# Two row maxima of a later group moved behind the shift rows, with the score banks in one ring, in a hash-masked attention and expert kernel

## The chip, the core and the metric

The kernel runs on one core of a Trainium2 chip. The core has engines that run side by side and meet only through semaphores: TensorE (PE in the profile, with PEld for loading its stationary operand), VectorE (DVE), ScalarE (ACT), GpSimd (POOL), and SyncE (SP), which here only issues DMA transfers. TensorE writes to PSUM, which has eight banks of 512 fp32 columns on 128 partitions; VectorE and ScalarE read PSUM, GpSimd doesn't. Everything else lies in SBUF. The metric is the device time of one execution in microseconds; the median of several runs is compared.

## What is computed

The attention has 4 batches of 8 heads, 768 positions and head size 64. A query may see a key only where the six sign bits of both (their products with a small matrix proj) agree. The attended values of the eight heads form a row of 512 for each of 3072 tokens; each row goes to the one expert of eight whose gate product is largest, through two matrix products with a ReLU between, and is scaled by the gate's probability.

```python
q_bits = (np.einsum('bhsd,dk->bhsk', q, proj) > 0).astype(np.int64)
k_bits = (np.einsum('bhsd,dk->bhsk', k, proj) > 0).astype(np.int64)
...
mask = q_bucket[:, :, :, None] == k_bucket[:, :, None, :]
scores = scale * np.matmul(q, k.transpose(0, 1, 3, 2))
scores = np.where(mask, scores, -1000000000.0)
scores = scores - np.max(scores, axis=-1, keepdims=True)
attn = np.exp(scores)
attn = attn / (np.sum(attn, axis=-1, keepdims=True) + 1e-09)
return np.matmul(attn, v).astype(np.float32)
...
expert_idx = np.argmax(logits, axis=1)
...
h = np.maximum(xe @ w1[e], 0.0)
ye = h @ w2[e]
out[mask] = gate_w[mask, None] * ye
```

## The kernel before

**Groups.** Attention works on pairs of heads, 16 in all, and each pair in two groups of 384 queries: t = 2 × pair + half, 32 groups. The loop over t is written out by hand, and the instructions of TensorE, VectorE and ScalarE keep the order in which they are written (line 762). GpSimd's and SyncE's instructions are ordered by the framework's scheduler. A group stands in the loop as follows.

- presum with VectorE (L277), then what is put at slot "w", then the product with v of the group before (`av`, L308 and L311) into a bank o, then its column sums (`sums`, L287, turned by L290).
- Then a string of letters (L784) that sets the order of the rest: m is a row maximum of the next group (`maximum`, L228 two products into a pair of banks, L229 the reduction), p is a piece of this group (`piece`, L267 and L268 into one bank, L270 the exponential), e evacuates o, i inverts the sums (`invert`, L296 to L298), x turns the product with v into token rows (L339, L340), s makes the shift rows of the next group, digits call what was put at that slot.
- A group has twelve pieces (two heads of six key blocks) and needs six maxima (two heads of three query blocks). After pieces 3, 5 and 9 GpSimd adds exponentials together (L275, L277), which the column sums need.

**Shift rows.** `shift_rows` takes the six maxima of a group, marks rows without a partner (L241), puts the negated maximum beside the marks (L242), turns both with four transposes (L245, L246) into the bank "misc", copies two parts of it out (L249 rows, L250 marks) and sends the rows by DMA into the last row of the operand qa (L252), where the pieces of that group read them.

**Operands.** Each head has four operands of 768 columns in the fast fp32 form, qa, qb, ka and kb: high parts, low parts and code bits. `code_products` (L160) makes the products with proj of the next pair but one at the end of each odd group, `code_signs` (L164, L165) turns them to signs in cr at the start of the next even group, and `head_operands` sends eight pieces of cr by DMA into ka and qa (L176, L177), copies high parts (L178 to L181) and subtracts low parts (L182, L183).

**Banks.** Two pairs of banks take the maxima (ps_s), two single banks the pieces (ps_t), one the product with v (ps_o), and one everything else (ps_m, "misc"): sums, codes, shift rows, token rows, gate products. A bank is taken again when its last reader is done.

After the loop the last group is finished in three parts (L804 to L824), the experts are sorted, and the expert stage follows.

## Time and profile before

| | us |
|---|---|
| median of 3 runs (lowest, highest) | 930.82 (926.26, 930.95) |
| profiled execution, whole | 925.8 |
| its span, from the first to the last instruction | 924.0 |
| TensorE busy | 822.1 (89%) |
| VectorE busy | 561.4 (61%) |
| GpSimd busy | 483.5 (52%) |
| ScalarE busy | 436.8 (47%) |

Busy times are sums over the span, and a busy TensorE isn't TensorE at its peak: its clock is granted in steps, and the profile gives the granted clock beside the busy time of any stretch. In a timeline each row has its start, its length, the engine, the line of the kernel, the operation, what it writes and reads, how many instructions of that kind follow each other, and in brackets how long the engine stood idle before and what ended that. An instruction that waits for a shared resource after it has started shows that as length, not as idle time. Where a row has a count, its length runs from the first to the last of them.

### The profile page before, as it was taken

Reading aid. Unit: us, or ns where it says so; the run is one execution under the profiler, and the core shown is the slowest. Engines: PE = TensorE matmul, PEld = TensorE weight load, DVE = VectorE, ACT = ScalarE, POOL = GpSimd, SP = SyncE. Lnnn points to the kernel's source line nnn. Section 1 sums busy time; section 2 is a strip of 40 time slices with the busy share of each in tenths; the row PEclk is TensorE's granted clock in tenths of the full one; section 3 lists DMA queues with packets and bytes.
Section 4 is the critical chain, followed back from the end, with each engine's and each line's share of the span. In section 5 each row is a group of like instructions: output and inputs, shape, how many; then the busy total and the mean of one; then the engine's idle time right before and its main releaser. Section 6 shows DMA issues by size and latency. Waiting matters only on the chain.

```text
span 924.0 us, 14353 instructions
## 1 busy us (share of the span) xinstructions
PE 822.1 (89%) x5175; PEld 586.9 (64%) x5175; DVE 561.4 (61%) x951; ACT 436.8 (47%) x816; POOL 483.5 (52%) x444
## 2 busy tenths in 40 slices
PE   4679898888988988889889898988999999999997
PEld 1444464455544545446445464547999999999995
DVE  5455466677654587556657865665756466567561
ACT  3545546545555464654645555343424334434440
POOL 3535546355654465564637566555036647545643
PEclk9877899888987989789888898889999999999999
DMA  7472021021310211302103040111664665655641
GB/s 215 134 234 62 21 71 59 20 75 42 103 59 21 73 58 53 94 22 72 58 19 103 14 142 25 26 67 60 181 166 133 184 167 149 187 167 168 197 137 44
DMA packets 55081, 89.67 MB, mean 97 GB/s; under 512 B 9330, under 2 KB 31438, under 8 KB 55000
## 3 DMA queue, kind: packets, MB, share of 16 engines
q1 hardware_dynamic: 47960, 75.86, 28.0%
q0 software_dynamic: 4992, 12.69, 3.9%
q8 instruction: 43, 0.70, 0.3%
q10 hardware_dynamic: 2048, 0.10, 0.1%
q14 instruction: 38, 0.31, 0.1%
HBM read 65.69 MB, written 20.37 MB: 93 GB/s over the span
## 4 chain that ended last, share of the span: by engine, by line
PE 41%; issue 20%; DVE 18%; POOL 13%; DMA 5%; ACT 2%; SPq 0%; POOLq 0%; DVEq 0%; ACTq 0%
PE o L311 16%; POOL y L968 8%; PE s L228 7%; DVE top L229 6%; PE t L267 4%; PE t L268 4%; DVE mt L241 3%; PE misc L287 3%; DMA y<-yo,tags 2%; PE misc L160 2%; PE misc L245 2%; DVE s L296 2%; DVE xr L340 1%; DMA xs<-xr,slot 1%; POOL yo L966 1%
## 5 line engine op out<-in xcount | busy, mean ns | idle before, releaser
L270 ACT ACTIVATE pt<-t 128x384 f32<-128x384 f32 x384 | 170.4, 488 | 121.7 <-PE t L268 116.5
L229 DVE TENSOR_REDUCE top<-s 128x1 f32<-128x768 f32 x192 | 174.7, 946 | 18.5 <-PE s L228 13.3
L275 POOL TENSOR_TENSOR ps<-pt 128x768 f32<-128x768 f32 x64 | 116.5, 1820 | 125.7 <-ACT pt L270 117.3
L311 PE MATMUL o<-pt,vt 128*64 128x384 f32 (+1 forms) x816 | 181.2, 609 | 0.0
L267 PE MATMUL t<-qa,ka 77*128 77x384 f32 x384 | 149.9, 390 | 6.2 <-ACT pt L270 6.2
L268 PE MATMUL t<-qb,kb 128*128 128x384 f32 x384 | 133.6, 348 | 0.0
L311 PEld LDWEIGHTS o<-pt,vt 128*64 128x64 f32 x816 | 70.1, 177 | 97.9 <-issue 97.7
L968 POOL DMA_INDIRECT y<-yo,tags x89 | 103.2, 1159 | 25.2 <-issue 22.6
L228 PE MATMUL s<-ka,qa 76*128 76x512 f32 (+1 forms) x384 | 105.3, 371 | 7.3 <-DVE top L229 2.4
L267 PEld LDWEIGHTS t<-qa,ka 77*128 77x128 f32 x384 | 74.4, 194 | 43.9 <-ACT pt L270 28.1
L183 POOL TENSOR_TENSOR qb<-raw,qa 64x768 fp32r<-64x768 f32 x30 | 55.4, 1863 | 73.6 <-DVE qa L179 67.4
L290 DVE STREAM_TRANSPOSE st<-misc 128x192 f32<-128x192 f32 x32 | 12.2, 382 | 132.7 <-PE misc L287 132.6
L228 PEld LDWEIGHTS s<-ka,qa 76*128 76x128 f32 x384 | 66.9, 199 | 28.1 <-DVE top L229 12.0
L648 DVE TENSOR_TENSOR wlo<-wraw,whi 128x1024 fp32r<-128x1024 f32 x60 | 73.5, 1226 | 16.7 <-ACT whi L643 15.9
L959 PE MATMUL hps<-hh,wlo 128*128 128x436 f32 (+6 forms) x224 | 76.4, 341 | 0.6 <-issue 0.6
L959 PE MATMUL hps<-hl,whi 128*128 128x436 f32 (+6 forms) x224 | 76.3, 341 | 0.0
L959 PE MATMUL hps<-hh,whi 128*128 128x448 f32 (+10 forms) x224 | 76.3, 341 | 0.0
L926 ACT ACTIVATE hh<-hps 128x352 fp32r<-128x352 f32 (+3 forms) x56 | 27.9, 499 | 101.8 <-PE hps L940 94.2
L268 PEld LDWEIGHTS t<-qb,kb 128*128 128x128 f32 x384 | 75.7, 197 | 0.0
L940 PE MATMUL hps<-xh,whi 128*128 128x352 f32 (+3 forms) x224 | 75.0, 335 | 0.0
L940 PE MATMUL hps<-xh,wlo 128*128 128x428 f32 (+6 forms) x224 | 74.8, 334 | 0.0
L940 PE MATMUL hps<-xl,whi 128*128 128x428 f32 (+6 forms) x224 | 74.8, 334 | 0.0
(231 smaller groups left out, 1374.3 us busy)
## 6 DMA issues: line engine op xcount, KB each, us to landing
wraw<-w SPq DMA_DIRECT2D x64, 512.0 KB
raw<-qk SPq DMA_DIRECT2D x30, 384.0 KB
xs<-zrow SPq DMA_DIRECT2D x8, 910.0 KB
vt<-v SPq DMA_DIRECT2D x16, 384.0 KB
vr<-vt SPq DMA_DIRECT2D x16, 384.0 KB
xr<-xs SPq DMA_DIRECT2D x12, 178.8 KB
xr<-xs SPq DMA_DIRECT2D x8, 227.5 KB
y<-yo,tags POOLq DMA_INDIRECT x89
```

Source lines behind the costliest of these rows:

```text
L183: G.tensor_tensor(out=qb[D:P], in0=raw[0:D], in1=bf(qa[0:D]), op=ALU.subtract)
L228: PE.matmul(out=s[:, c0:c1], lhsT=qa[0:KM, qs], rhs=ka[0:KM, c0:c1], start=True, stop=True)
L229: V.reduce_max(out=tops[t][:, i:i + 1], in_=s[:, 0:S], axis=AX.X)
L267: PE.matmul(out=s[:, 0:384], lhsT=ka[0:KM + 1, ks], rhs=qa[0:KM + 1, qs], start=True, stop=False)
L268: PE.matmul(out=s[:, 0:384], lhsT=kb[:, ks], rhs=qb[:, qs], start=False, stop=True)
L270: A.activation(pt[:, kc], s[:, 0:384], AF.Exp, bias=0.0, scale=0.125)
L275: eng.tensor_tensor(out=ps, in0=pt[:, 0:2], in1=pt[:, 2:4], op=ALU.add)
L311: PE.matmul(out=o[hh * D:hh * D + D, qs], lhsT=vt[:, kc, hh * D:hh * D + D], rhs=pts[t][hh][:, kc, qs], start=False, stop=kc == NB - 1)
L648: loeng.tensor_tensor(out=lo[:, i:i + step], in0=cell["t"], in1=bf(hi[:, i:i + step]), op=ALU.subtract)
L940: PE.matmul(out=hps[:, 0:w], lhsT=wt[:, c, fs], rhs=xt[:, c, 0:w], start=n == 0, stop=n == 3 * NDC - 1)
L959: PE.matmul(out=yps[:, 0:w], lhsT=wt[:, f, ds], rhs=ht[:, 0:w], start=n == 0, stop=n == 3 * NFC - 1)
L968: rows_apart("out", G.indirect_dma_start(out=out_seg, out_offset=bass.IndirectOffsetOnAxis(ap=tags[:, i, 0:1].bitcast(I32), axis=0), in_=y ...
```

## The change

- The string of the loop is rewritten. A group now computes maxima 2 to 5 of the next group among its pieces (m) and maxima 0 and 1 of the group after that behind the shift rows (M). The first two of group 1 stand ahead of the loop. Slots 1 to 5 move accordingly.
- The bank of the product with v joins the ring of the pieces: ps_t has three banks, ps_o is gone.
- The marks (L241) and the first operation of the inversion (L296) take their constant from a column of a table in SBUF, as an operation with two tensors.
- The code products move from the end of an odd group to its second slot, and their signs on VectorE follow at once; the scaling on ScalarE stays at the start of the even group.
- The high part of qa is cast on ScalarE instead of VectorE. The casts and subtractions for kb, and the cast for qb, are split off and move to the start of the odd group.
- The DMA of the shift rows is issued from SyncE instead of ScalarE.

```diff
@@ -72,7 +72,7 @@
     ident = const.tile([P, P], F32, name="ident")
     pj2 = const.tile([P, 2, SQ], F32, name="pj2")
     pj = pj2[:, 0]
-    cols = const.tile([P, 6], F32, name="cols")
+    cols = const.tile([P, 8], F32, name="cols")
     wg_sb = const.tile([P, NPAIR, 32], F32, name="wg_sb")
     eoff = const.tile([P, 3, E], F32, name="eoff")
     ids = const.tile([P, B * NB + 7, NG], I32, name="ids")
@@ -101,8 +101,7 @@
     smp = att.enter_context(tc.tile_pool(name="smp", bufs=6))
     gp = att.enter_context(tc.tile_pool(name="gp", bufs=2))
     ps_s = psa.enter_context(tc.tile_pool(name="ps_s", bufs=2, space=PSUM))
-    ps_t = psa.enter_context(tc.tile_pool(name="ps_t", bufs=2, space=PSUM))
-    ps_o = psa.enter_context(tc.tile_pool(name="ps_o", bufs=1, space=PSUM))
+    ps_t = psa.enter_context(tc.tile_pool(name="ps_t", bufs=3, space=PSUM))
     ps_m = psa.enter_context(tc.tile_pool(name="ps_m", bufs=1, space=PSUM))
 
 
@@ -162,25 +161,32 @@
     def code_signs(pr):
         cr = codes[pr] = codep.tile([P, 384], F32R, name="cr")
         V.tensor_scalar(out=cr, in0=cps_of.pop(pr)[:, 0:384], scalar1=0.0, scalar2=cols[:, 0:1], op0=ALU.is_gt, op1=ALU.subtract)
+
+    def code_scale(pr):
+        cr = codes[pr]
         A.activation(cr, bf(cr), AF.Copy, bias=0.0, scale=cols[:, 1:2])
 
     def new_operands():
         return [opp.tile([P, S], F32R, name=n) for n in ("qa", "qb", "ka", "kb")]
 
-    def head_operands(pr, hh):
+    def head_first(pr, hh):
+
         raw, cr = raws_of[pr][hh], codes[pr]
-        qa, qb, ka, kb = new_operands()
-        operands[2 * pr + hh] = (qa, qb, ka, kb)
+        qa, qb, ka, kb = operands[2 * pr + hh] = new_operands()
         for x in range(2):
             r, cs = SQ * (2 * hh + x), slice(384 * x, 384 * x + 384)
             SY.dma_start(out=bf(ka[D:D + NC1, cs]), in_=bf(cr[r + NC1:r + 2 * NC1]))
             SY.dma_start(out=bf(qa[D:KM, cs]), in_=bf(cr[r:r + NCODE]))
         A.copy(out=ka[0:D], in_=raw[D:P])
-        V.tensor_copy(out=qa[0:D], in_=raw[0:D])
+        A.copy(out=qa[0:D], in_=raw[0:D])
+        G.tensor_tensor(out=qb[D:P], in0=raw[0:D], in1=bf(qa[0:D]), op=ALU.subtract)
+
+    def head_second(pr, hh):
+        raw = raws_of[pr][hh]
+        qa, qb, ka, kb = operands[2 * pr + hh]
         A.copy(out=kb[D:P], in_=raw[D:P])
+        G.tensor_tensor(out=kb[0:D], in0=raw[D:P], in1=bf(kb[D:P]), op=ALU.subtract)
         A.copy(out=qb[0:D], in_=raw[0:D])
-        G.tensor_tensor(out=kb[0:D], in0=raw[D:P], in1=bf(kb[D:P]), op=ALU.subtract)
-        G.tensor_tensor(out=qb[D:P], in0=raw[0:D], in1=bf(qa[0:D]), op=ALU.subtract)
 
     KM = D + NCODE
 
@@ -238,7 +244,8 @@
         mt = mts[t % 2]
         top = tops[t].rearrange("p (h j) -> p j h", h=2)[:, :, h0:h1]
         marks = mt[:, :, 0:6].rearrange("p j (c h) -> p j c h", c=3)[:, :, :, h0:h1]
-        V.tensor_scalar(out=marks, in0=top.unsqueeze(2).broadcast_to([P, 3, 3, h1 - h0]), scalar1=-0.5 * BIG, scalar2=None, op0=ALU.is_le)
+        V.tensor_tensor(out=marks, in0=top.unsqueeze(2).broadcast_to([P, 3, 3, h1 - h0]),
+                        in1=cols[:, 6:7].unsqueeze(2).unsqueeze(3).broadcast_to([P, 3, 3, h1 - h0]), op=ALU.is_le)
         V.scalar_tensor_tensor(out=mt[:, :, SQ + h0:SQ + h1], in0=bf(mt[:, :, h0:h1]), scalar=-DROP, in1=top, op0=ALU.mult, op1=ALU.subtract)
         rp = ps_m.tile([P, 512], F32, name="misc")
         for jj in range(3):
@@ -249,7 +256,7 @@
         A.copy(out=r, in_=rp[SQ:SQ + 2, 0:384])
         A.copy(out=shifts[t], in_=rp[0:6])
         for hh in hhs:
-            A.dma_start(out=bf(operands[2 * pr + hh][0][KM:KM + 1, 384 * g:384 * g + 384]), in_=bf(r[hh:hh + 1, 0:384]))
+            SY.dma_start(out=bf(operands[2 * pr + hh][0][KM:KM + 1, 384 * g:384 * g + 384]), in_=bf(r[hh:hh + 1, 0:384]))
 
     pts = {}
     psums = {}
@@ -293,7 +300,7 @@
     def invert(t, inv):
         s = sums_of.pop(t).rearrange("p (h j) -> p h j", h=2)
         s6 = smp.tile([P, 2, 3], F32, name="s6", bufs=2)
-        V.tensor_scalar(out=s6, in0=s, scalar1=0.0, scalar2=float(S), op0=ALU.is_equal, op1=ALU.mult)
+        V.scalar_tensor_tensor(out=s6, in0=s, scalar=0.0, in1=cols[:, 7:8].unsqueeze(2).broadcast_to([P, 2, 3]), op0=ALU.is_equal, op1=ALU.mult)
         V.scalar_tensor_tensor(out=s6, in0=s6, scalar=1e-9, in1=s, op0=ALU.add, op1=ALU.add)
         V.reciprocal(out=inv, in_=s6)
 
@@ -659,7 +666,7 @@
             t = ps_s.tile([P, 1024], F32, name="s")
             first_h.extend((t[:, 0:512], t[:, 512:1024]))
         elif f > 3:
-            pool, name = ((ps_o, "o"), (ps_t, "t"), (ps_m, "misc"), (ps_t, "t"))[f - 4]
+            pool, name = ((ps_t, "t"), (ps_t, "t"), (ps_m, "misc"), (ps_t, "t"))[f - 4]
             first_h.append(pool.tile([P, 512], F32, name=name))
         return first_h[f]
 
@@ -697,16 +704,17 @@
 
     for e in range(E):
         put(1 + e // 2, 3 + e % 2, partial(prefill, e))
-    put(0, 1, partial(code_products, 1))
+    put(0, 1, partial(code_products, 1), partial(code_signs, 1))
     for pr in range(NPR):
         t, w = 2 * pr, "w" if pr else 1
         if pr + 1 < NPR:
-            put(t, w, partial(code_signs, pr + 1), partial(head_operands, pr + 1, 0), partial(head_operands, pr + 1, 1))
+            put(t, w, partial(code_scale, pr + 1), partial(head_first, pr + 1, 0), partial(head_first, pr + 1, 1))
             put(t, 2, partial(load_v, pr + 1))
-            put(t + 1, "w", partial(sum_v, pr + 1))
+            put(t + 1, "w", partial(head_second, pr + 1, 0), partial(head_second, pr + 1, 1), partial(sum_v, pr + 1))
         if pr + 2 < NPR:
             put(t, 2, partial(load_raw, pr + 2))
-            put(t + 1, 6, partial(code_products, pr + 2))
+            put(t + 1, 2, partial(code_products, pr + 2), partial(code_signs, pr + 2))
+
     def start_route(t):
         b, g = t // (2 * NPAIR), t % 2
         r = route(b, g)
@@ -773,18 +781,22 @@
     shift_rows(0, (1,))
     first_q(0, 1)
     first_q(1, 1)
+    maximum(1, 0)
+    maximum(1, 1)
     for t in range(NT):
         if t:
             presum(t - 1, 1, 1, V)
             run_at(t, "w")
-            o = ps_o.tile([P, 512], F32, name="o")
+            o = ps_t.tile([P, 512], F32, name="t")
             av(t - 1, o)
             sums(t - 1)
         nm = np_ = 0
-        for x in "mmepp0mpp1mppi2mp3pmp4pxpps56":
-            if x == "m" and t + 1 < NT:
-                maximum(t + 1, nm)
+        for x in "epp1mpp2mipp3mpp4mppxp5psMM6":
+            if x in "mM":
                 nm += 1
+                u, i = (t + 1, nm + 1) if nm < 5 else (t + 2, nm - 5)
+                if u < NT:
+                    maximum(u, i)
             elif x == "s" and t + 1 < NT:
                 shift_rows(t + 1)
             elif x == "p":
@@ -803,7 +815,7 @@
     assert not at
     t = NT - 1
     presum(t, 1, 1, V)
-    o = ps_o.tile([P, 512], F32, name="o")
+    o = ps_t.tile([P, 512], F32, name="t")
     inv2, (c0, c1, c2) = last_route(t, o)
     av(t, o, slice(0, P))
     c0.pop(0)()
@@ -1159,7 +1171,9 @@
     a["w2"] = np.ascontiguousarray(moe_w2.reshape(E, F, NG, NDC, SQ).transpose(0, 1, 3, 2, 4).reshape(E, F, DM))
     a["ident"] = np.eye(P, dtype=np.float32)
     a["tri"] = np.triu(np.ones((P, P), np.float32), 1)
-    cols = np.zeros((P, 6), np.float32)
+    cols = np.zeros((P, 8), np.float32)
+    cols[:, 6] = -0.5 * BIG
+    cols[:, 7] = S
     cols[:, 1] = cols[:, 3] = 1.0
     cols[0:D, 4] = cols[D:P, 5] = 1.0
     for r in range(0, P, SQ):
```

## The prediction

> **What bounds the kernel now.** I read the page first, then one windows view by stage.
>
> ```profile
> span 924.0 us, 14353 instructions
> ...
> PEclk9877899888987989789888898889999999999999
> ```
>
> ```profile
> 49.70:620.00 570.30, 498.08 (x3300) 290.61 (x3302) 364.38 (x598) 302.30 (x596) 315.24 (x276) 0.86 0.20 62
> 620.00:924.00 304.00, 294.72 (x1802) 281.16 (x1792) 171.84 (x312) 112.55 (x184) 146.55 (x144) 0.99 0.52 149
> ```
>
> The columns are length, then busy time of PE, PEld, DVE, ACT, POOL, then granted clock, DMA share, GB/s. The expert stage (from 620) has PE at 97% and a clock of 0.99; the diff touches nothing in it. The 32 groups of the attention loop take 570.3 us with PE busy 498.1, so it idles 72.2 us there, and the clock is 0.86. All that the change can win is in those two numbers. The list of waits says what the idle time is:
>
> ```profile
> PE misc L245 <- DVE mt L242: 51.6, 33, 2.3
> PE misc L160 <- ACT marks L250: 16.2, 14, 1.2
> PE t L267 <- ACT pt L270: 6.2, 5, 5.3
> ```
>
> Two waits make most of it: the transposes of the shift rows wait for mt (1.56 us each), and the code products wait for the evacuation of the only "misc" bank (1.16 us each, 14 times: every odd group up to t = 27). To see what makes mt late I read the timeline of an even group, from the end of the column sums to the next product with v:
>
> ```profile
> 265.77 0.98 PE L228 MATMUL s<-ka,qa 76*128 76x512 f32 x4
> 266.43 3.68 DVE L229 TENSOR_REDUCE top<-s 128x1 f32<-128x768 f32 x4
> 266.59 0.35 PE L267 MATMUL t<-qa,ka 77*128 77x384 f32 x1
> ...
> 269.45 1.84 POOL L275 TENSOR_TENSOR ps<-pt 128x768 f32<-128x768 f32 x1 [2.03 <-ACT pt L270]
> ...
> 272.10 0.88 ACT L270 ACTIVATE pt<-t 128x384 f32<-128x384 f32 x2 [0.33 <-PE t L268]
> ...
> 273.18 1.81 POOL L275 TENSOR_TENSOR ps<-pt 128x768 f32<-128x768 f32 x1
> ...
> 273.31 0.34 PE L268 MATMUL t<-qb,kb 128*128 128x384 f32 x1
> ...
> 273.84 1.18 DVE L241 TENSOR_SCALAR mt<-top 128x18 fp32r<-128x18 f32 x1
> 275.05 0.17 DVE L242 SCALAR_TENSOR_TENSOR mt<-mt,top 128x6 fp32r<-128x6 f32 x1
> 275.37 0.49 PE L245 MATMUL misc<-ident,mt 128*34 128x128 f32 x3 [1.71 <-DVE mt L242]
> ...
> 275.89 0.35 PE L308 MATMUL o<-marks 6*64 6x384 bf16 x2
> ```
>
> Take Z = 265.77, where PE has finished the sums. PE runs through the two first maxima (0.82 us), twelve pieces and four maxima, and is done at Z + 7.88. POOL makes three additions back to back from Z + 3.68 to Z + 9.22. The 18-element L241 starts at Z + 8.07 and ends at Z + 9.25, 0.03 after POOL's last addition: it does not compute for 1.18 us, it waits for POOL. So mt is bound by **the first addition on POOL plus three additions**, and PE's transposes follow 5.92 us after that first addition starts. The odd group adds the code products:
>
> ```profile
> 282.68 0.97 PE L228 MATMUL s<-ka,qa 76*128 76x512 f32 x4
> ...
> 292.22 0.49 PE L245 MATMUL misc<-ident,mt 128*34 128x128 f32 x3 [1.66 <-DVE mt L242]
> ...
> 293.34 0.57 ACT L250 CAST marks<-misc 6x512 bf16<-6x512 f32 x1
> ...
> 293.97 1.51 PE L160 MATMUL misc<-raw,pj 128*32 128x384 f32 x8 [1.16 <-ACT marks L250]
> ...
> 295.41 0.53 PE L308 MATMUL o<-marks 6*64 6x384 bf16 x2
> ```
> ```profile
> 302.93 0.96 PE L228 MATMUL s<-ka,qa 76*128 76x512 f32 x4
> ```
>
> From Z to the product with v are 10.12 us in the even group and 12.73 in the odd one; the product and sums then take 6.79 us (275.89 to 282.68) and 7.52 (295.41 to 302.93). The pair takes 37.16 us. Why 7.52 and not 6.79 is in the windows view, cut at the steps of the granted clock:
>
> ```profile
> 273.13:276.55 3.42, 1.71 (x12) 0.81 (x13) 3.01 (x5) 1.41 (x4) 1.86 (x2) 1.00 0.01 2
> 276.55:279.96 3.41, 3.41 (x14) 1.43 (x12) 0.00 (x0) 1.45 (x3) 1.11 (x7) 0.50 0.14 14
> ...
> 290.20:293.62 3.42, 0.95 (x6) 0.35 (x5) 2.71 (x5) 1.62 (x4) 1.64 (x1) 1.00 0.00 0
> 293.62:297.03 3.41, 3.06 (x14) 0.85 (x16) 1.48 (x3) 1.10 (x3) 0.18 (x1) 0.50 0.01 1
> 297.03:300.44 3.41, 3.41 (x14) 1.23 (x12) 0.06 (x1) 3.34 (x5) 3.41 (x2) 0.50 0.07 17
> ```
>
> A window of 3.41 us in which PE was busy 1.71 is followed by one at half clock. The odd group's longer idle time is followed by two. Half a window of PE work, 1.7 us, is lost in each fully used one.
>
> **The change part by part.** The sum is made against the profiled execution: 925.8 us, of which 924.0 are the span. The median of the runs is 930.82, 0.5% above.
>
> *Maxima ahead.* Two maxima leave the front of the group (0.82 us on PE from 265.77 to 266.59) and stand behind the shift rows. Nothing is computed less. In front, the pieces and POOL's first addition come 0.82 earlier: Z + 2.86, so the transposes stand at Z + 2.86 + 5.92 = 8.78, and PE, done at 7.06, still waits 1.7. Behind, the transposes (275.37 to 275.89, 0.52) and the moved maxima (0.82) bring the product with v to Z + 10.12. That is the time of before: **gain in an even group 0**. VectorE does these two reductions in the product's time, where it did nothing (0.00 busy in 276.55:279.96). In front it has 1.84 us less to do (two of the four in 3.68). It gains less than that, because the inversion still meets POOL's first addition; I put its arrival at L241 at about Z + 7.4 in place of 8.07. POOL's last addition ends at 2.86 + 5.54 = Z + 8.40, so it waits there. What is late next is therefore POOL, not VectorE.
>
> *Two-tensor forms.* L241 and the first operation of the inversion (L296) read a column instead of a constant. The rows to compare are operations with two tensors in SBUF that met POOL:
>
> ```profile
> L241 DVE TENSOR_SCALAR mt<-top x33: 155/1190/1481, 12.5 to 608.6; 128x18 fp32r<-128x18 f32 x31, 128x9 fp32r<-128x9 f32 x2
> ```
> ```profile
> L277 DVE TENSOR_TENSOR ps<-ps,pt x32: 949/957/2936, 48.2 to 631.6; 128x768 f32<-128x768 f32 x32
> ```
> ```profile
> L382 DVE TENSOR_TENSOR oh<-oh,eoff x7: 183/184/1740, 184.2 to 629.7; 128x24 f32<-128x24 f32 x7
> ```
> ```profile
> 335.05 3.69 POOL L183 TENSOR_TENSOR qb<-raw,qa 64x768 fp32r<-64x768 f32 x2 [5.02 <-DVE qa L179]
> ...
> 337.04 1.74 DVE L382 TENSOR_TENSOR oh<-oh,eoff 128x24 f32<-128x24 f32 x1
> ```
>
> L382 takes 0.18 us alone and 1.74 beside POOL, ending at 338.78 with POOL's instruction (338.74). The two-tensor form waits just as L241 does, so I take **0**; the other end is that L241 falls to its 0.16 us, a rival below. The Trainium skill agrees with these rows in "SBUF — State Buffer", section "Who interferes with whom": a VectorE instruction with two SBUF inputs contends with a GpSimd one that reads SBUF. Its page "VectorE: DVE Perf Modes", section "Mode 2×_2P", says only that tensor_tensor cannot use both read ports for one tensor; whoever reads no further expects the wait to go, and by that the sum would be the rival's.
>
> *Code products.* In 14 odd groups they move from the end (wait 1.16, then 1.51 at half clock) to the second slot, between pieces, at full clock: about 0.75, an estimate, half of 1.51. There they delay pieces 4 to 9. POOL's last addition needs the exponentials that ended at 272.98, Z + 7.21; in the new order they end at 7.21 − 0.82 + 0.75 = 7.14, where POOL is free at 2.86 + 3.73 = 6.59: 0.55 lost. The product with v stands at Z + 10.12 + 0.55 = 10.67 instead of 12.73: 2.06 gained. PE is done at 7.06 + 0.75 and waits until 8.78 + 0.55; this wait of 1.5 us resembles the even group's, so I take one half-clock window, not two: 7.52 becomes 6.79, 0.73 gained. **14 × 2.79 = 39 us.** The signs follow on VectorE:
>
> ```profile
> 295.55 0.62 DVE L164 TENSOR_SCALAR cr<-misc,cols 128x384 fp32r<-128x384 f32 x1 [2.61 <-DMA qa<-rows]
> ```
>
> These 0.62 us stand in front of L241, which then starts at about Z + 8.0 and has until 8.95 under POOL. Without that cover they would cost up to 14 × 0.62 = 8.7.
>
> *Casts.*
>
> ```profile
> L178 ACT CAST ka<-raw 64x768 fp32r<-64x768 f32 x30 | 24.9, 830 | 0.7
> ```
> ```profile
> L179 DVE CAST qa<-raw 64x768 fp32r<-64x768 f32 x30 | 15.9, 569 | 0.0
> ```
>
> qa goes from VectorE (0.57) to ScalarE (0.83 like ka's), and kb and qb move an odd group later. ScalarE has 4 × 0.83 in either group in place of 6 and 0, POOL two subtractions in either in place of four and none; both lie under the product's 6.8 us. Only in group 0 do they stand in front of the exponentials (the wait of 5.3 in the list above): 2 × 0.83 = **1.7 us gained** once. Without the cover, 0.83 × 30 = 25 us would be lost.
>
> *Third bank in the ring.* PE waits for a bank visibly only 6.2 us in all, 5.3 of them that first one, and POOL's chain hides the rest: 0, at most about 0.2 per group.
>
> *Rows on SP.*
>
> ```profile
> 335.04 0.81 SPq L176 DMA_DIRECT2D ka<-cr  x1
> ...
> 340.83 0.73 SPq L177 DMA_DIRECT2D qa<-cr  x1
> ```
> ```profile
> L252 ACTq DMA_DIRECT2D qa<-rows x64: 504/524/1531, 14.5 to 612.1; - x64
> ```
>
> ScalarE's queue loses 2 × 0.52 us per group, hidden. On SP the two transfers stand beside eight issues that take 6.5 us. Ahead of them they cost nothing; behind them, see the last rival. I take 0, since the rows are ready before the codes.
>
> Sum: 39 + 1.7 = 41; 925.8 − 41 = 885.
>
> **Rivals.**
>
> *The clock stays up (831 to 866).* The remaining wait is 1.5 to 1.7 us. Where it straddles two windows, neither shows 1.71 busy and no half clock follows. All 32 escaping would save 32 × 1.7 = 54 (831), half of them 27 (858). For it: the idle time is shorter than before in odd groups. Against it: the even group's 1.71 triggered it. By the Trainium skill, "TensorE: Matmul & The Clock Gate", section "Why this matters for your kernels", only gaps above about 3 us bring half rate, which would give 831; the trace shows half rate after a wait of 1.71.
>
> *The two-tensor form does not wait (about 783).* L241 would end about Z + 7, 1.5 us earlier, the wait fall to some 0.2, and the half clock go: 32 × (1.5 + 1.7) = 102, 885 − 102 = 783. Against it: the rows of L277 and L382.
>
> *Two half windows remain (about 902).* If the wait's tail reaches into the slow window, an odd group still loses 0.73 to 1.7: 14 × 1.2 = 17.
>
> *No difference (about 926).* The change does not do what it says: the third maximum, the signs and the inversion keep VectorE, not POOL, ahead of mt, by the 2.8 us that an odd group gained; nothing is left but group 0's 1.7, which is within what can be told.
>
> *Slower: rows queue behind the codes on SP (about 943).* If SP takes the rows after the eight codes, they are issued some 9.8 us after the transposes (1.7 to the end of marks, 0.6 for the scale, 6.5 for the codes, 1.0 of their own) and land about 2.2 later (an estimate: marks begin at 293.34 as the rows' cast ends, and L164 above is released by their landing at 295.55); the first piece wants them at 0.52 + 0.82 + 6.79 = 8.1. That is 3.9 us in 15 even groups: +58. It decides from an issue later than 5.9 us after the transposes.
>
> **How the numbers follow.** Forecast 0.56 (866 to 900), clock up 0.16, two-tensor 0.06, two half windows 0.09, no difference 0.06, slower 0.07. Leaving out two-tensor, no difference and slower (0.19) the range is 835 to 920. Faster by over 0.5% 0.87, within 0.06, slower 0.07; 0.5% is what runs of before differ by (926.26 to 930.95) and about what can be told. I give 885.
>
> **What would show it.** Right: L241 still near 1.2 us and ending with POOL's addition; no wait of L160 for L250; one half-clock window per group; pairs of about 34.3 us; the stage from 620 on as long as now. Wrong: a first piece that waits for qa's rows (SP), L241 at 0.2, or a clock above 0.9 in the attention stage.

## The result, and the profile after

The change made the kernel faster. In the first series its median is 892.85 us (four runs, 889.81 to 901.97) against 928.54 before, a ratio of 0.9633 with a 95% interval of 0.9553 to 0.9714. In a second series, beside partial versions, it is 886.27 us (six runs, 883.01 to 886.62) against 922.17: 0.9592 (0.9565 to 0.9618). The forecast was 885.

The profile is that of a run of the second series (886.62 us). Its page, the heading and the parts on busy time and granted clock:

```profile
span 884.8 us, 14398 instructions
...
PE 781.6 (88%) x5175; PEld 593.2 (67%) x5175; DVE 551.8 (62%) x921; ACT 457.1 (52%) x846; POOL 493.1 (56%) x444
...
PEclk9899989988999898988998899889999999999999
```

The windows view from the start of the first to the start of the last product with v (the third part of the last group's), and behind it, of the kernel before and then of the changed one. Its columns are length, then busy time of PE, PEld, DVE, ACT, POOL, then granted clock, DMA share, GB/s.

```profile
49.23:637.52 588.29, 513.06 (x3447) 301.07 (x3447) 371.58 (x629) 309.18 (x611) 325.06 (x284) 0.86 0.20 62
637.52:924.00 286.48, 280.21 (x1647) 270.84 (x1646) 164.64 (x281) 106.03 (x168) 136.74 (x136) 1.00 0.54 153
```

```profile
45.55:599.10 553.55, 473.16 (x3443) 306.33 (x3443) 366.77 (x602) 330.86 (x642) 336.30 (x287) 0.89 0.22 69
599.10:884.00 284.90, 279.22 (x1647) 271.00 (x1646) 164.32 (x281) 106.00 (x168) 139.09 (x136) 0.99 0.54 155
```

The loop is 34.7 us shorter, what stands before it 3.7, and what stands behind it, up to the end of the span, 0.8. In the loop PE's busy time fell by 39.9 us for the same products, while its idle time rose from 75.2 to 80.4 (length less busy). The gain in the loop is a higher clock, not less waiting. The waits say the same:

```profile
PE misc L252 <- DVE mt L249: 76.6, 32, 5.3
```

The code products (now L159) no longer stand in PE's list of waits, and no wait for the shift rows' transfer does; the wait for mt rose from 51.6 to 76.6 us. The timeline of an even group (Z = 101.97) and the odd one behind it (Z = 118.64) shows what mt waits for:

```profile
106.56 1.85 POOL L284 TENSOR_TENSOR ps<-ps,pt 128x768 f32<-128x768 f32 x1
...
108.37 1.80 POOL L282 TENSOR_TENSOR ps<-pt 128x768 f32<-128x768 f32 x1
...
109.02 1.19 DVE L247 TENSOR_TENSOR mt<-top,cols 128x18 fp32r<-128x18 f32 x1
...
110.56 0.49 PE L252 MATMUL misc<-ident,mt 128*34 128x128 f32 x3 [2.38 <-DVE mt L249]
...
111.78 0.35 PE L315 MATMUL t<-marks 6*64 6x384 bf16 x2
...
120.54 0.85 PE L159 MATMUL misc<-raw,pj 128*32 128x384 f32 x8
```

L247, the former L241, starts under POOL's last addition and ends with it (110.21 and 110.17), in its form with two tensors too. The code products take 0.85 us in place of 1.51, at full clock.

For the experiments I read the end of the column sums of every group off each timeline, and sum up by pairs of groups. **Plain pairs** are eight without routing. **Route pairs** are six in which the gate and the sorting of a finished batch stand (t = 7 to 10, 15 to 18, 23 to 26). "Start" is the first product with v. "Half" counts windows of 3.41 us at half clock in the loop, from the clock in the trace. The ratios leave out runs at a lower granted clock that took over 1.5% more than the fastest of their kernel (three of the six with the casts back, one in each of three other rows), and the last four columns of the row marked * come from such a run, of 854 us where the others took 841 to 852, so they aren't compared with other rows.

| kernel | ratio to before (95%) | plain pairs, mean us | route pairs, mean us | start | half |
|---|---|---|---|---|---|
| before | 1 | 36.9 | 38.5 | 49.2 | 49 |
| changed | 0.9592 (0.9565, 0.9618) | 32.9 | 38.1 | 45.6 | 37 |
| codes alone | 0.9840 (0.9815, 0.9865) | 34.8 | 38.5 | 49.2 | 39 |
| changed, codes back | 0.9797 (0.9752, 0.9843) | 35.0 | 38.1 | 46.0 | 45 |
| changed, casts back | 0.9873 (0.9830, 0.9915) | 35.9 | 37.7 | 50.1 | 45 |
| changed, banks back | 0.9750 (0.9713, 0.9788) | 34.4 | 37.8 | 47.2 | 40 |
| changed, constants and rows back | 0.9565 (0.9521, 0.9608) | 33.1 | 36.7 | 46.3 | 34 |
| changed, maxima back | 0.9546 (0.9518, 0.9573) | 34.0 | 35.7 | 45.2 | 32 |
| the same, casts back too | 0.9661 (0.9613, 0.9708) | 34.4 | 35.0 | 48.8 | 35 |
| before, third addition on VectorE | 0.9271 (0.9225, 0.9316) | 31.6 | 36.6 | 48.0 | 21 |
| changed, third addition on VectorE * | 0.9125 (0.9099, 0.9150) | 29.5 | 37.3 | 45.6 | 33 |
| maxima back, third addition on VectorE | 0.8759 (0.8732, 0.8786) | 28.4 | 32.2 | 45.4 | 8 |
| the same, sums of v first | 0.8831 (0.8795, 0.8868) | 28.7 | 32.5 | 45.0 | 12 |

Differences between kernels are given by the ratio, where one point is 9.2 us (a hundredth of the median of before in these series, 922.17 to 923.09). The half windows and pairs are those of one execution each. Of the half windows, 23 stand in plain and 18 in route pairs before, 12 and 18 in the changed kernel.

### The profile page after: what moved, and what is told of

The parts are those of the page before. It is cut to its first block, busy times and chain, and to the rows that moved or that the text cites. A ratio compares the mean times of both kernels' runs of the same rounds, so it can differ in the third digit from the quotient of the medians.

```text
span 900.2 us, 14398 instructions
## 1 busy us (share of the span) xinstructions
PE 799.1 (89%) x5175; PEld 601.0 (67%) x5175; DVE 553.0 (61%) x921; ACT 457.9 (51%) x846; POOL 493.1 (55%) x444
## 4 chain that ended last, share of the span: by engine, by line
PE 41%; DVE 22%; issue 19%; POOL 11%; DMA 4%; ACT 1%; SPq 1%; another core or an unknown queue 0%; POOLq 0%; ACTq 0%; DVEq 0%
PE t L318 18%; POOL y L980 9%; DVE top L235 7%; PE s L234 6%; DVE mt L247 4%; PE t L274 4%; PE t L275 3%; PE misc L294 2%; PE misc L252 2%; DVE s L303 2%; DVE xr L347 2%; DMA y<-yo,tags 2%; PE misc L159 1%; POOL yo L978 1%; PE t L315 1%
## 5 line engine op out<-in xcount | busy, mean ns | idle before, releaser
L235 DVE TENSOR_REDUCE top<-s 128x1 f32<-128x768 f32 x192 | 177.3, 949 | 74.0 <-PE s L234 72.5
L318 PE MATMUL t<-pt,vt 128*64 128x384 f32 (+1 forms) x816 | 182.7, 614 | 0.0
L274 PE MATMUL t<-qa,ka 77*128 77x384 f32 x384 | 140.8, 367 | 2.3 <-ACT pt L277 2.3
L318 PEld LDWEIGHTS t<-pt,vt 128*64 128x64 f32 x816 | 70.8, 178 | 98.3 <-issue 98.0
L234 PE MATMUL s<-ka,qa 76*128 76x512 f32 (+1 forms) x384 | 112.4, 393 | 4.8 <-ACT qa L217 2.0
L188 POOL TENSOR_TENSOR kb<-raw,kb 64x768 fp32r<-64x768 f32 x30 | 64.8, 2180 | 50.4 <-ACT kb L187 43.0
L234 PEld LDWEIGHTS s<-ka,qa 76*128 76x128 f32 x384 | 72.4, 215 | 28.4 <-issue 11.1
L252 PE MATMUL misc<-ident,mt 128*34 128x128 f32 x99 | 19.3, 312 | 74.4 <-DVE mt L249 74.4
```

What stands on the lines that cost most here:

```text
L188: G.tensor_tensor(out=kb[0:D], in0=raw[D:P], in1=bf(kb[D:P]), op=ALU.subtract)
L234: PE.matmul(out=s[:, c0:c1], lhsT=qa[0:KM, qs], rhs=ka[0:KM, c0:c1], start=True, stop=True)
L235: V.reduce_max(out=tops[t][:, i:i + 1], in_=s[:, 0:S], axis=AX.X)
L274: PE.matmul(out=s[:, 0:384], lhsT=ka[0:KM + 1, ks], rhs=qa[0:KM + 1, qs], start=True, stop=False)
L318: PE.matmul(out=o[hh * D:hh * D + D, qs], lhsT=vt[:, kc, hh * D:hh * D + D], rhs=pts[t][hh][:, kc, qs], start=False, stop=kc == NB - 1)
```

## The experiments

Theory: POOL's additions bound mt, and the move of the code products is nearly all of the gain. Rivals: another part brings it, or VectorE bounds mt.

**The codes back in their old place**, from the changed kernel:

```diff
-put(t, w, partial(code_scale, pr + 1), ...
+put(t, w, *([partial(code_signs, pr + 1)] if pr else []), partial(code_scale, pr + 1), ...
-put(t + 1, 2, partial(code_products, pr + 2), partial(code_signs, pr + 2))
+put(t + 1, 6, partial(code_products, pr + 2))
```

> The changed kernel, but the code products stand at the end of the odd groups and the signs at the start of the even ones again, as before the change; all else of the change stays. Theory (the move of the code products is nearly the whole gain): 14 odd groups lose 2.06 to 2.8 us each, so 29 to 39 us of the 36 us gained go: about 920 to 930 us, ratio to the kernel before 0.99 to 1.00; pairs of groups of about 36.5 to 37.2 us, and the wait of the code products for the bank of the shift rows is there again. Rival A (the third bank in the ring, the casts or the moved maxima bring a good part): at most 900 to 910 us, ratio 0.970 to 0.985.

Measured: 903.37 us, 0.9797. That is 2.05 points, 19 us, above the changed kernel: rival A. Plain pairs give back 2.1 us each, route pairs nothing.

**The codes alone**, from the kernel before:

```diff
-    A.activation(cr, bf(cr), AF.Copy, bias=0.0, scale=cols[:, 1:2])
+
+def code_scale(pr):
+    cr = codes[pr]
+    A.activation(cr, bf(cr), AF.Copy, bias=0.0, scale=cols[:, 1:2])
-put(0, 1, partial(code_products, 1))
+put(0, 1, partial(code_products, 1), partial(code_signs, 1))
-put(t, w, partial(code_signs, pr + 1), partial(head_operands, ...
+put(t, w, partial(code_scale, pr + 1), partial(head_operands, ...
-put(t + 1, 6, partial(code_products, pr + 2))
+put(t + 1, 2, partial(code_products, pr + 2), partial(code_signs, pr + 2))
```

> The kernel before with one part of the change alone: code products and signs at the second slot of the odd group. Maxima, casts, banks, rows and constant forms are those of before. Theory (the move of the code products is nearly the whole gain): 14 x (2.06 to 2.79) = 29 to 39 us less than before, ratio 0.958 to 0.97. Rival A (it needs the other parts: casts off VectorE and maxima off the front make the room): the signs and casts now delay mt, ratio 0.975 to 1.0.

Measured: 908.21 us, 0.984: 15 us. The ratio is in rival A's range. The windows of the first six plain groups and of the four route groups behind them, of this kernel, and then of the kernel before:

```profile
55.84:161.54 105.70, 94.62 (x632) 56.13 (x631) 64.87 (x95) 59.74 (x117) 58.25 (x51) 0.89 0.25 77
161.54:239.02 77.48, 66.14 (x456) 38.62 (x455) 56.62 (x100) 41.40 (x82) 44.82 (x40) 0.89 0.20 66
```

```profile
57.03:167.78 110.75, 95.99 (x632) 56.08 (x631) 64.98 (x95) 60.04 (x117) 58.01 (x51) 0.88 0.23 70
167.78:245.98 78.20, 67.19 (x455) 40.10 (x455) 55.26 (x100) 41.73 (x82) 45.08 (x39) 0.87 0.20 66
```

Three plain pairs gain 5.05 us, two route pairs 0.7. The timeline of the first of these route groups (Z = 161.54) shows a part of the reason:

```profile
168.27 0.85 PE L364 MATMUL misc<-ot,wg_sb 128*32 128x384 f32 x8 [0.88 <-DVE cr L164]
```

The gate product takes the only "misc" bank next after the code products and waits until VectorE has read the signs out of it. The exponentials come later by that too, and POOL's third addition starts at Z + 10.13, in place of 8.28 in the same group before; in plain odd groups it is 8.03 in place of 7.29. PE waits so in three of the twelve route groups. So the move works as predicted where nothing else stands, and the route pairs take the gain back. The part put at 39 us is worth 15 to 19, and some 20 must come from parts put at nothing.

**The casts back**: four casts and four subtractions of a pair in the even group, the cast of qa on VectorE.

```diff
-A.copy(out=qa[0:D], in_=raw[0:D])
+V.tensor_copy(out=qa[0:D], in_=raw[0:D])
-put(t, w, ..., partial(head_first, pr + 1, 0), partial(head_first, pr + 1, 1))
+put(t, w, ..., partial(head_first, pr + 1, 0), partial(head_second, pr + 1, 0), partial(head_first, pr + 1, 1), partial(head_second, pr + 1, 1))
-put(t + 1, "w", partial(head_second, pr + 1, 0), partial(head_second, pr + 1, 1), partial(sum_v, pr + 1))
+put(t + 1, "w", partial(sum_v, pr + 1))
```

> The changed kernel, but the four casts and the four subtractions of a pair's heads all stand in the even group again, with the cast of qa on VectorE. Theory (they lie beside the product with v; only group 0 pays): 0 to 3 us slower than the changed kernel, ratio to it 1.000 to 1.003. Rival (four subtractions in a row on POOL delay POOL's first addition, and the second addition on VectorE waits for them, as in the route groups): 15 to 25 us slower, since code products, maxima and what the first runs show leave some 25 us of the gain to the casts, the bank, the rows and the constants.

Measured: 909.95 to 914.81 us in the three runs that aren't left out, 0.9873: 2.8 points, 26 us. The timeline of this kernel around Z = 72.98 shows the mechanism where it is worst:

```profile
67.81 0.35 PE L315 MATMUL t<-marks 6*64 6x384 bf16 x2
...
70.17 1.01 DVE L181 CAST qa<-raw 64x768 fp32r<-64x768 f32 x2
...
70.68 2.19 POOL L188 TENSOR_TENSOR kb<-raw,kb 64x768 fp32r<-64x768 f32 x1 [4.49 <-DMA ka<-cr]
...
72.94 3.63 POOL L182 TENSOR_TENSOR qb<-raw,qa 64x768 fp32r<-64x768 f32 x2
...
76.65 1.87 POOL L188 TENSOR_TENSOR kb<-raw,kb 64x768 fp32r<-64x768 f32 x1
...
78.59 1.82 POOL L282 TENSOR_TENSOR ps<-pt 128x768 f32<-128x768 f32 x1
...
80.92 1.40 DVE L247 TENSOR_TENSOR mt<-top,cols 128x18 fp32r<-128x18 f32 x1
82.25 1.80 POOL L282 TENSOR_TENSOR ps<-pt 128x768 f32<-128x768 f32 x1
82.36 1.71 DVE L249 SCALAR_TENSOR_TENSOR mt<-mt,top 128x6 fp32r<-128x6 f32 x1
...
84.21 0.80 PE L252 MATMUL misc<-ident,mt 128*34 128x128 f32 x3 [4.58 <-DVE mt L249]
```

VectorE casts qa only behind the moved maxima and its own addition. POOL subtracts for kb first here and starts 2.9 us behind the product with v; the four subtractions reach to Z + 5.5. POOL's first addition starts at Z + 5.6 in place of Z + 2.7 (104.65 − 101.97 in the changed kernel's trace), and both operations that make mt wait for an addition each. The transposes start at Z + 11.2.

Of the eight even groups of plain pairs, two are like this; there the product and sums took only 5.2 us, at full clock. In two they took 6.8 us, and the subtractions reach to Z + 3.8. In four they took 7.4 to 8.1 us, partly at half clock, and the first addition starts at Z + 2.7 as in the changed kernel. So the faster the product with v runs, the less it covers. The loop also starts 4.5 us later.

**The banks back**: two in the ring, one for the product with v.

```diff
-ps_t = ...(name="ps_t", bufs=3, space=PSUM)
+ps_t = ...(name="ps_t", bufs=2, space=PSUM)
+ps_o = ...(name="ps_o", bufs=1, space=PSUM)
...
-o = ps_t.tile([P, 512], F32, name="t")
+o = ps_o.tile([P, 512], F32, name="o")
```

> The changed kernel with two banks in the ring of the pieces and one of its own for the product with v again. Theory (a third bank is hidden by POOL's chain of additions): the changed kernel's time within 4 us. Rival (PE runs ahead of ScalarE with the third bank and is done with the pieces earlier, and so starts the maxima and the shift rows earlier): 10 to 25 us slower; pieces end about 0.5 to 1 us later after the sums.

Measured: 898.87 us, 0.975: 1.6 points, 14.6 us. The rival. In plain groups the pieces end at Z + 7.86 and 7.08 (odd and even) in place of 7.17 and 6.20, the transposes start at Z + 9.46 and 8.78 in place of 8.96 and 8.57. The loop also starts 1.7 us later.

**Constants and rows back**, two parts that the prediction put at nothing, undone together:

```diff
-V.tensor_tensor(out=marks, in0=top..., in1=cols[:, 6:7]..., op=ALU.is_le)
+V.tensor_scalar(out=marks, in0=top..., scalar1=-0.5 * BIG, scalar2=None, op0=ALU.is_le)
-V.scalar_tensor_tensor(out=s6, in0=s, scalar=0.0, in1=cols[:, 7:8]..., op0=ALU.is_equal, op1=ALU.mult)
+V.tensor_scalar(out=s6, in0=s, scalar1=0.0, scalar2=float(S), op0=ALU.is_equal, op1=ALU.mult)
-SY.dma_start(out=bf(operands[2 * pr + hh][0][KM:KM + 1, ...
+A.dma_start(out=bf(operands[2 * pr + hh][0][KM:KM + 1, ...
```

> The changed kernel with two parts undone that the prediction put at nothing: the comparison L247 and the first operation of the inversion take a constant again in place of a second tensor, and the rows' transfers stand on ScalarE's queue again. Theory: the changed kernel's time within 4 us, ratio to before 0.955 to 0.964, L247 still near 1.2 us. Rival (the forms with two tensors do not wait for POOL, those with a constant do): 10 us or more slower, ratio above 0.970, L247 longer by 0.3 us or more.

Measured: 883.10 us, 0.9565. Its interval overlaps that of the changed kernel: no difference that can be told. The lines view by source line (shortest, median, longest ns) of this kernel, then of the changed one:

```profile
L247 DVE TENSOR_SCALAR mt<-top x33: 158/1500/2131, 12.4 to 567.8; 128x18 fp32r<-128x18 f32 x31, 128x9 fp32r<-128x9 f32 x2
```

```profile
L247 DVE TENSOR_TENSOR mt<-top,cols x33: 160/1200/2134, 12.4 to 573.2; 128x18 fp32r<-128x18 f32 x31, 128x9 fp32r<-128x9 f32 x2
```

Both forms take 0.16 us when POOL is still and over 1 us beside it. The median of 1.5 for the constant is what the rival expected of L247, but the time isn't: the length is whatever is left of POOL's addition.

**The maxima back in front**:

```diff
-for x in "epp1mpp2mipp3mpp4mppxp5psMM6":
+for x in "MMepp1mpp2mipp3mpp4mppxp5ps6":
-u, i = (t + 1, nm + 1) if nm < 5 else (t + 2, nm - 5)
+u, i = t + 1, nm - 1
-maximum(1, 0)
-maximum(1, 1)
```

> The changed kernel with the two first maxima of the next group at the front of the group again, not ahead of the product with v. Theory (the maxima only change places on PE; POOL's chain of three additions bounds mt either way): same time as the changed kernel within 5 us, ratio to before 0.958 to 0.969, POOL's first addition about 0.8 us later after the sums, the transposes about 0.7 later, and the product with v where it was. Rival (the moved maxima are the gain, since VectorE came too late for mt): ratio above 0.975, and L247 falls to less than 0.5 us because VectorE comes after POOL's last addition.

Measured: 880.35 us, 0.9546, faster than the changed kernel by 0.46 points with intervals that just touch. The net is 4 us against the moved maxima, and it hides two larger parts: moved, they win 1.1 us in each plain pair and lose 2.4 in each route pair. The lines view from 49.7 to 590 us, of the kernel with the maxima back and then of the changed one:

```profile
L188 POOL TENSOR_TENSOR kb<-raw,kb 64x768 fp32r<-64x768 f32 x29 | 52.2, 1815 | 51.1 <-ACT kb L187 26.1 <-DMA xs<-xr,slot 13.8 <-issue 11.2
L284 DVE TENSOR_TENSOR ps<-ps,pt 128x768 f32<-128x768 f32 x31 | 29.6, 956 | 6.0 <-POOL ps L282 6.0
```

```profile
L188 POOL TENSOR_TENSOR kb<-raw,kb 64x768 fp32r<-64x768 f32 x29 | 62.4, 2172 | 46.2 <-ACT kb L187 38.9 <-issue 7.3
L284 DVE TENSOR_TENSOR ps<-ps,pt 128x768 f32<-128x768 f32 x30 | 34.9, 1163 | 0.0
```

Behind the two moved reductions (1.82 us), VectorE's addition L284 comes when POOL subtracts, and both become longer.

**Maxima and casts back**, the last but with the edit of the casts besides:

> The changed kernel with the two first maxima in front (880 us, ratio 0.955) and, besides, the casts and the four subtractions all in the even group, qa's cast on VectorE. Theory (four subtractions of 1.85 us in a row reach past the sums, POOL's first addition comes about 2 us late, in every even group): 20 to 33 us slower than 880, ratio 0.975 to 0.99. Rival (they hurt only together with the moved maxima, since VectorE's additions then fall beside them): ratio 0.955 to 0.965.

Measured: 892.84 us, 0.9661: 1.15 points, 11 us, between the theory and its rival. Its timeline where a plain group's product with v begins:

```profile
101.62 0.45 PE L315 MATMUL t<-marks 6*64 6x384 bf16 x2
101.73 1.02 DVE L181 CAST qa<-raw 64x768 fp32r<-64x768 f32 x2
...
102.51 3.67 POOL L182 TENSOR_TENSOR qb<-raw,qa 64x768 fp32r<-64x768 f32 x2 [1.80 <-DVE qa L181]
```

With the maxima in front VectorE casts qa at once, and POOL starts 0.9 us behind the product with v. In plain groups it is done by Z + 1.4 to 3.1, ahead of its first addition (Z + 3.6 to 3.8). So the casts are worth about 11 us by themselves, and 26 beside moved maxima. Of the 11, 3.6 lie before the first product with v (the profiled run is the fastest, 886.79); where the rest lies the trace doesn't show. Nor was it tried whether qa's cast or the place of the subtractions counts for more.

**POOL's third addition on VectorE**, from the kernel before and no part of the change. It stands beside the product with v, where VectorE has little else to do:

```diff
-presum(t - 1, 1, 1, V)
+presum(t - 1, 1, 0, V)
+presum(t - 1, 1, 1, V)
...
-if np_ in (3, 5, 9):
+if np_ in (3, 5):
```

> The kernel before with one edit that is no part of the change: POOL's third addition of the sums stands on VectorE at the start of the next iteration. Theory (POOL's last addition bounds mt in the kernel before too, by about 1.2 us a group): the transposes come about 1.2 us earlier in 32 groups (38 us), and part of the 49 half-clock windows of 1.7 us goes (0 to 40 us): ratio to before 0.915 to 0.96. Rival (VectorE, with its four reductions behind the sums, bounds mt in the kernel before, and POOL's chain comes to bind only through the change): ratio 0.985 to 1.0.

Measured: 858.61 us, 0.9271: 7.3 points, 67 us, more than the whole change. POOL's additions bound mt before the change too. The lines view of L241, and the timeline of an even group (Z = 239.73), of this kernel:

```profile
L241 DVE TENSOR_SCALAR mt<-top x33: 158/165/1631, 12.5 to 549.7; 128x18 fp32r<-128x18 f32 x31, 128x9 fp32r<-128x9 f32 x2
```

```profile
245.26 1.86 POOL L277 TENSOR_TENSOR ps<-ps,pt 128x768 f32<-128x768 f32 x1
...
247.72 0.17 DVE L241 TENSOR_SCALAR mt<-top 128x18 fp32r<-128x18 f32 x1
...
248.24 0.49 PE L245 MATMUL misc<-ident,mt 128*34 128x128 f32 x3 [0.75 <-DVE mt L242]
```

POOL is done at Z + 7.39 and L241 takes its 0.17 us; PE waits 0.75 in place of 1.71. The half-clock windows fall from 49 to 21.

**The same edit in the changed kernel**:

> The changed kernel with POOL's third addition of the sums given to VectorE, at the start of the next iteration ahead of VectorE's own one, where VectorE has only the two moved maxima. Theory (POOL's last addition holds mt): L247 runs in about 0.2 us when POOL is idle, mt comes 1.2 to 1.5 us earlier in each of 32 groups, PE's wait before the transposes falls to below 0.8 us, and most of the half-clock windows of the attention stage go: 50 to 90 us less than the changed kernel, about 800 to 845 us, ratio to before 0.86 to 0.91. Rival (VectorE itself bounds mt by then: its third maximum, the inversion and the signs): mt comes at most 0.5 us earlier, ratio 0.94 to 0.965. Second rival (the extra addition on VectorE delays the sums): PE waits for VectorE ahead of the column sums, ratio above 0.965.

Measured: 842.90 us, 0.9125, just outside the range of the ratio. L247 falls to 0.17 us in plain groups; in the profiled run, of 854 us, plain pairs take 29.5 us and route pairs 37.3. The timeline beside the product with v ahead of Z = 112.89 shows the new collision:

```profile
108.84 0.95 DVE L282 TENSOR_TENSOR ps<-pt 128x768 f32<-128x768 f32 x1
108.86 5.12 POOL L188 TENSOR_TENSOR kb<-raw,kb 64x768 fp32r<-64x768 f32 x2 [3.87 <-ACT kb L187]
109.89 2.41 DVE L284 TENSOR_TENSOR ps<-ps,pt 128x768 f32<-128x768 f32 x1
```

Behind the moved reductions, both of VectorE's additions stand beside POOL's subtractions.

**The same edit with the maxima back in front**:

> The third addition of the sums on VectorE, as in the run of 842.9 us, and the two first maxima at the front of the group again. Theory (the moved maxima delay VectorE's additions, and the product with v by 0.7 us behind the shift rows): faster than with the maxima moved by 5 to 15 us: 828 to 838 us, ratio to before 0.895 to 0.907. Rival (with POOL's third addition gone, VectorE bounds mt, and there the moved maxima are what helps: two reductions of 0.95 us less between the sums and mt): 10 to 40 us slower, 853 to 880 us, and L247 runs in 0.2 us behind a late third maximum.

Measured: 807.96 us, 0.8759, 114 us less than before and the fastest of all. Neither the theory's range nor the rival's holds it. The clock on its page:

```profile
PEclk9999999999999999999999988999999999999999
```

Eight half-clock windows are left. Against the kernel with the maxima back alone, transposes 1.0 to 1.45 us earlier in some 30 groups (8.44 and 8.51 in place of 9.90 and 9.53) and 24 windows of 1.7 us fewer make 37 + 41 = 78 us; measured are 7.9 points, 73. Next to this, the moved maxima of the change cost 34 us.

**The sums of v first**, one further edit: `sum_v` ahead of `head_second` at slot "w" of the odd group.

> The kernel of 808 us (third addition on VectorE, maxima in front) with the sums of v ahead of the second casts and subtractions in the odd groups. In that kernel the second product of the shift rows waits in three route groups for 2.2 us for POOL's last small operation on v, which stands behind a subtraction and a gather. Theory: that wait goes, 3 x 2.4 = 7 us less and perhaps the half-clock window of these groups: 798 to 803 us, ratio 0.865 to 0.871. Rival (the subtractions, 1 us later on POOL, push its first addition back): same time or slower, ratio 0.875 to 0.885.

Measured: 816.64 us, 0.8831, slower by 0.7 points: the rival. The waits of the kernel without the edit, and then with it:

```profile
PE misc L253 <- POOL v L151: 6.7, 3, 2.2
```

```profile
POOL vh L149 <- ACT vr L146: 45.0, 12, 3.9
PE misc L253 <- POOL v L151: 2.8, 1, 2.8
```

The wait of three route groups becomes one. But POOL, which waited for ScalarE's casts ahead of its subtractions (46.8 us, 12 times, without the edit), now waits for ScalarE's sums of v there, and in most plain odd groups the subtractions start at about Z − 1.6 in place of Z − 2.9. In a route group (timeline of the kernel with the edit, Z = 288.13) the last one stands where the first addition belongs, and mt is made behind that addition, 12 us past Z:

```profile
296.26 1.81 POOL L188 TENSOR_TENSOR kb<-raw,kb 64x768 fp32r<-64x768 f32 x1 [2.19 <-ACT pt L277]
...
298.29 1.80 POOL L282 TENSOR_TENSOR ps<-pt 128x768 f32<-128x768 f32 x1
298.48 1.65 DVE L247 TENSOR_TENSOR mt<-top,cols 128x18 fp32r<-128x18 f32 x1
```

## Why the prediction was right, and where it was wrong

The forecast of 885 us holds: 886 and 893. The sum behind it was 41 us; 34 to 38 were measured (3.67 and 4.08 points). But its terms don't hold, and their errors cancel, so that the total came out is luck. Taken out of the changed kernel one at a time, codes, casts, bank and maxima are worth 19, 26, 15 and −4 us. That is 56 in all, so they don't simply add up either.

**What bounds the kernel** was right. mt comes with POOL's last addition, and taking that addition away is worth 67 us in the kernel before. The stage behind the loop stayed as it was, within 0.8 us.

**Code products, 39 us: mis-sized.** Measured 15 and 19. In plain pairs the step was right: an odd group from Z to the product with v takes 8.96 + 1.23 = 10.19 us (forecast 10.67), the product and sums 6.86 (6.79), and a pair with the codes alone 34.4, as 37.16 − 2.79 says. What failed is the factor: "14 × 2.79" took one plain pair for all, and six of the pairs stand beside routing, where 0.0 was gained (38.5 and 38.5). Eight times 2.1 is 17.

**Casts, 1.7 us: mis-sized, the cover was wrong.** Measured 11 without and 26 with the moved maxima. What stands before the first product with v alone gives 3.6. The prediction said that POOL's subtractions lie under the product's 6.8 us whether two or four stand there. In the kernel before, the four end 1.2 to 2.8 us past Z in plain even groups; they cost nothing only because the first addition starts as late as Z + 3.6. The moved maxima take that room from both sides: the addition starts at Z + 2.7, and the subtractions begin 1.4 to 2 us later behind the product with v than with the maxima in front. In the worst two groups the subtractions reach to Z + 5.5. The two edits belong together.

**Third bank, 0: wrong, 14.6 us.** "POOL's chain hides the rest" fails: with two banks the pieces end up to 0.9 us later. In plain odd groups POOL's third addition, which needs the tenth piece, starts at Z + 7.26 in place of 6.77; in even groups the first already starts 0.2 later, and the chain behind it. The prediction's own sentence that in odd groups the third addition starts 0.55 late for want of exponentials had shown that pieces bound there.

**Maxima, 0: right as a net (4 us lost), by two errors.** Plain pairs gain 1.1 us each: the product with v comes 0.25 us earlier behind Z in either group, not 0, and the rest is three fewer half-clock windows in the eight pairs. Route pairs lose 2.4 each, 1.7 of them by six more half-clock windows (18 in place of 12): the prediction put VectorE's reductions "in the product's time, where it did nothing", read from one plain group. That this is why the route pairs lose is read from the lines above, not tried alone.

**Two-tensor forms, 0, and rows on SP, 0: right,** as far as undoing both at once can tell. No piece waits for the rows, so the slower rival fell. The rival at 783 us, a form that doesn't wait for POOL, fell: L247 still ends with the addition.

**The half clock** was right in size: one window less in each of 14 odd groups would be 35 in place of 49; 37 were counted. But of the 12 windows that went, 11 lay in plain pairs and none in route pairs. The rival of a clock that stays up fell: the loop's is 0.89.

**What it left out:** the new string puts slot 5 ahead of the shift rows, and with it the expert weights' first cast in the last groups. The timeline of the changed kernel, Z = 542.41:

```profile
549.40 1.71 DVE L652 CAST whi<-wraw 128x1024 fp32r<-128x1024 f32 x1
...
551.18 2.34 POOL L655 TENSOR_TENSOR wlo<-wraw,whi 128x1024 fp32r<-128x1024 f32 x1 [0.63 <-DVE whi L652]
551.42 2.13 DVE L247 TENSOR_TENSOR mt<-top,cols 128x18 fp32r<-128x18 f32 x1
...
553.90 0.80 PE L252 MATMUL misc<-ident,mt 128*34 128x128 f32 x3 [5.29 <-DVE mt L249]
```

In the kernel before, the cast (L645) stands behind mt. This last pair takes 40.9 us in place of 37.2. That the order is the cause is read from the rows; it wasn't tried alone. Nor was it tried alone what takes the gain of the route pairs back.

## What to carry to other kernels

Price a moved step in every kind of iteration that the trace has, since a gain from the quiet ones is given back where other work already fills the gap. When two engines hold each other up at a shared resource, move the work into a time when one of them is idle rather than change the form of the instruction. Take a change of many parts apart on the chip even when its total comes out as forecast: here one part cost time, two were worth more than their cover let them seem, and a single other edit was worth more than the whole.

## What the hardware showed

- **The wait goes both ways.** In the changed kernel with the third addition on VectorE, VectorE's addition began at 108.84, 0.02 us ahead of POOL's subtractions, and took its 0.95 us; the two subtractions took 5.12 in place of twice 1.82. Whichever starts first runs, the other waits until that instruction ends. The Trainium skill says this in "SBUF — State Buffer", section "SBUF: two separate sides": an exclusive lock, held for the whole instruction, and no sharing of bandwidth. The rows agree.
- **It isn't a matter of one or two tensors.** L247 waits with a constant (median 1.50 us) and with a tensor (1.20), and a wait may follow a wait (1.40 and 1.71 in the kernel with the casts back).
- **Where the clock falls.** In the changed kernel PE waits 1.79 us (odd) and 2.37 (even) ahead of the transposes in plain groups, and 12 of the 16 have a half-clock window. In the fastest kernel it waits 0.33 and 1.34, and no plain group has one. But a wait of that size doesn't settle it. In the changed kernel with the third addition on VectorE (the run of 854 us), seven plain even groups wait 1.24 to 1.36 us, four with a half-clock window and three without. The windows view at the steps of the clock, of this kernel and then of the fastest:

```profile
132.85:136.27 3.42, 2.08 (x15) 1.26 (x16) 2.25 (x6) 1.89 (x5) 0.36 (x1) 1.00 0.02 5
136.27:139.68 3.41, 3.41 (x14) 1.32 (x12) 3.31 (x4) 3.34 (x5) 2.60 (x2) 0.51 0.01 1
```

```profile
127.70:131.11 3.41, 2.08 (x16) 1.36 (x16) 3.27 (x7) 1.77 (x5) 1.35 (x1) 1.00 0.00 0
131.11:134.53 3.42, 3.42 (x22) 1.50 (x22) 0.84 (x1) 3.30 (x6) 1.61 (x1) 1.00 0.03 6
```

With PE busy 2.08 us in a window of 3.41, the next one runs at half clock in one kernel and at full clock in the other. Elsewhere a window with 1.73 busy keeps the clock (maxima back, 372.58), and one with 2.35 loses it (before, 529.13). What decides between them these runs don't show. A wait of 1.71 us before half clock, as in the prediction's even group, is far below the gap of some 3 us that the Trainium skill gives in "TensorE: Matmul & The Clock Gate", section "Why this matters for your kernels"; the measurement decides.
